# An opening ordered by hand, with heads in 126 columns and rows placed by stores

## The chip, the cores and the metric

One core of a Trainium2 chip runs the kernel. The metric is the device time of one execution in microseconds, as the median over runs.

## The reference

The computation is the forward pass and the gradients of a gated mix of two attention branches, on 2048 tokens of width 576 in bfloat16. Only branch A and the gate matter for this change:

```python
# A: 32 query heads of 18, one key and value head for all of them
q = (x @ wq).reshape(B, S, 32, 18).transpose(0, 2, 1, 3)
k, v = x @ wk, x @ wv
p = softmax(einsum('bhqd,bkd->bhqk', q, k) * 18 ** -0.5)
a = einsum('bhqk,bkd->bhqd', p, v)...reshape(B, S, 576) @ wo
# B: segments of 32 tokens with 8 memory rows carried from one to the next, 32 heads of 128
g = sigmoid((x * gate_w).sum(-1, keepdims=True))
out = g * a + (1 - g) * b
# and the gradients for x, wq, wk, wv, wo, mem0, Wq, Wk, Wv, Wo, gate_w from grad_out
```

For its backward pass branch A needs, per head, q and the gradient of the head's output: `da = g * grad_out` times the transpose of `wo`. Branch B needs `db = (1 - g) * grad_out`.

## The kernel before

The kernel is a row of stages, each with its own pools of SBUF and PSUM: an opening; the transposed weight Wo of branch B (`make_WoT`); the token projections of branch B (`b_proj`); branch A's forward sweep woven with B's chain over the segments; B's bulk work; A's second sweep woven with B's backward chain; the weight gradients; the end. The change lies in the opening and adds small stores to `b_proj`.

**The opening before.** `prep` loads x and grad_out as tokens by features (`xt`, `go`, 16 tiles of 128 tokens), transposes x into `xT` on TensorE (five 128 x 128 transposes a tile, evacuated by ScalarE), and takes the gate's dot product on VectorE (line 1601). When all 16 dots are there, one Exp gives the gate for all tokens (line 1609). Then it scales `go` by g into `xt` and by 1 - g into itself (line 1619), transposes both (`daT`, `dbT`), and stores xT, da, db and dbT to DRAM for later stages. `a_weights` loads Wq, Wk, Wv and Wo of branch A; it spreads each head's 18 columns over 32 (`wqp`, `woTp`: 16 pairs of heads, 64 columns a pair). `a_setup` makes the keys and values as columns (`KV`) and as rows (`VK`, `WK`) and from the largest key of each feature a weight `smneg`.

`a_qd_all` then runs over 16 pairs of heads and 4 blocks of 512 tokens. For one unit, TensorE fills rows 0 to 63 of one PSUM tile `a_pq` with q of the pair and rows 64 to 127 with its output gradient, five steps of the contraction each, side by side in the two column halves of the array. ScalarE takes the absolute value of it (line 1756), and one more product with `smneg` adds for each token and head a lower bound, - |q| times the largest keys, in row 18 of each group of 32 rows; the softmax later needs no maximum. VectorE casts the tile to `a_QDs` (line 1766, three buffers), and one store takes all 128 rows, zero rows among them, to `qs_dram` (line 1767; even blocks from SyncE's queue, odd ones from GpSimd's). In `qs_dram` a head pair and block has 128 rows of 512 values, of 1 KB each:

```
rows   0-17  q, first head     18  its bound     19-31  zero
rows  32-49  q, second head    50  its bound     51-63  zero
rows  64-81  output gradient, first head         82-95  zero
rows 96-113  output gradient, second head       114-127 zero
```

`setup_A_consts` and `setup_B_consts` make masks and selection matrices, mostly on GpSimd, and `load_Wo` loads Wo of branch B (4.7 MB, half from each queue). In this stage the instructions of each engine are put in order by a scheduler; the stages behind it have an order written out by hand (`tc.manual_schedule()`), in which each engine runs its instructions as the program lists them.

**Behind it.** `proj_load` loads tiles `p_x` of dbT and xT. `make_WoT` transposes Wo (`w_ptr`, `WoT`) and stores it (line 637). `b_proj` does 31 items of 128 tokens: products into eight PSUM tiles `p_pb`, evacuated by VectorE and ScalarE to `p_tok` (line 77 and 79, two buffers), stored by SyncE one item later (lines 239 and 258). Its function `extra(n)` is called at item n and loads Wk and Wv at items 1 to 10 and Wq at item 16, then first memory rows and `load_A_kv`, which begins to read `qs_dram`. `load_v` (line 392) loads a tile `c_vx` in the sweep behind: 32 tokens by 4096 values, taken as "r (c x) -> c r x" with four groups c.

A TensorE, VectorE, ScalarE or GpSimd instruction whose line is a helper's carries that line: 82 for all products, 87 for transposes by `tr`, 77 and 79 for `evac` on VectorE and ScalarE.

Of the kernel before, what the change touches and what calls it, by code (L numbers as in the profile page):

```python
# [10 lines left out]
ALU = mybir.AluOpType  # L11
# [5 lines left out]
P = 128  # L17
# [29 lines left out]
class Kern:  # L47
# [1528 lines left out]
    def prep(self, keep, xk, sp, psum):  # L1576
        nc = self.nc
        T, NTT = self.T, self.NTT
        gwb = sp.tile([P, D], BF16, name="gwb")
# [3 lines left out]
        self.xT = xk.tile([P, NKT, T], BF16, name="xT")  # L1583
        self.daT = xk.tile([P, NKT, T], BF16, name="daT")
        dbT = sp.tile([P, NKT, T], BF16, name="dbT")
# [3 lines left out]
        for dst, src in ((xt, self.A_x), (go, self.grad_out)):  # L1589
            for q in range(4):  # L1590
                n0, n1 = q * NTT // 4, (q + 1) * NTT // 4
                nc.sync.dma_start(dst[:, n0:n1, :], src[n0 * P:n1 * P, :].rearrange("(n p) d -> p n d", p=P))
        xl = sp.tile([P, NTT, 2, 4, 16], BF16, name="xtail")
        tail_in = lambda t: t.rearrange("p (g c) -> p g c", c=GD)[:, :, P:GD].unsqueeze(1).to_broadcast([P, 2, 4, 16])
        tail = lambda tt: xl[:, tt].rearrange("p a g c -> p (a g c)")
        z = sp.tile([P, NTT], F32, name="z_all")
        for tt in range(NTT):
            for a in range(2):
                nc.scalar.copy(xl[:, tt, a], xt[:, tt, :].rearrange("p (g c) -> p g c", c=GD)[:, :, P:GD])
            junk = sp.tile([P, D], BF16, name="junk", bufs=2)  # L1600
            nc.vector.tensor_tensor_reduce(out=junk[:], in0=xt[:, tt, :], in1=gwb[:], scale=1.0, scalar=0.0,
                                           op0=ALU.mult, op1=ALU.add, accum_out=z[:, tt:tt + 1])
            tp = psum.tile([P, 6, P], BF16, name="trx", bufs=4)
            for kt in range(4):
                nc.tensor.transpose(tp[:, kt, :], xt[:, tt, GD * kt:GD * kt + P], self.identB[:])
            nc.tensor.transpose(tp[:, 4, :], tail(tt), self.identB[:])
            self.evac(self.xT[:, :, tt * P:(tt + 1) * P], tp[:, 0:5, :], use="s")
        ez = sp.tile([P, NTT], F32, name="ez")
        nc.scalar.activation(ez[:], z[:], ACT.Exp, scale=-1.0)
        nc.vector.tensor_scalar(out=ez[:], in0=ez[:], scalar1=1.0, scalar2=None, op0=ALU.add)  # L1610
        nc.vector.reciprocal(self.g_all[:], ez[:])
        nc.vector.tensor_scalar(out=self.omg_all[:], in0=self.g_all[:], scalar1=-1.0, scalar2=1.0,
                                op0=ALU.mult, op1=ALU.add)
        for kt in range(NKT):
            nc.gpsimd.dma_start(self.xT_dram[kt], self.xT[:, kt, :])
        for (dst, gcol, ddram, d4) in ((self.daT, self.g_all, self.da_dram, xt), (dbT, self.omg_all, self.db_dram, go)):
            for tt in range(NTT):
                d16 = d4[:, tt, :]
                nc.vector.tensor_scalar(out=d16, in0=go[:, tt, :], scalar1=gcol[:, tt:tt + 1], scalar2=None,
                                        op0=ALU.mult)  # L1620
                if tt % 4 == 3:
                    nc.gpsimd.dma_start(ddram[(tt - 3) * P:(tt + 1) * P, :].rearrange("(n p) d -> p n d", p=P), d4[:, tt - 3:tt + 1, :])
                tp = psum.tile([P, 6, P], BF16, name="trx", bufs=4)
                step = GD if dst is dbT else P
                for kt in range(4):
                    nc.tensor.transpose(tp[:, kt, :], d16[:, kt * step:kt * step + P], self.identB[:])
                if dst is dbT:
                    nc.gpsimd.tensor_copy(xl[:, tt], tail_in(d16))
                    nc.tensor.transpose(tp[:, 4, :], tail(tt), self.identB[:])
                else:  # L1630
                    nc.tensor.transpose(tp[:, 4, :], d16[:, D - P:D], self.identB[:])
                self.evac(dst[:, :, tt * P:(tt + 1) * P], tp[:, 0:5, :], use="v" if tt % 3 == 2 else "s")
        for kt in range(NKT):
            nc.gpsimd.dma_start(self.dbT_dram[kt], dbT[:, kt, :])

    def a_weights(self, keep, sp, psum):
        nc = self.nc
        wq = sp.tile([P, NKT, D], BF16, name="a_wq")
        wo = sp.tile([P, NKT, D], BF16, name="a_wo")
        wkv = keep.tile([P, NKT, P], BF16, name="a_wkv")  # L1640
        nc.gpsimd.memset(wkv[:], 0.0)
        self.wkv36 = keep.tile([P, NKT, 36], BF16, name="a_wkv36")
        for kt in range(NKT):
            rows = KT_ROWS[kt]
            r = slice(kt * P, kt * P + rows)
            nc.gpsimd.dma_start(wo[0:rows, kt, :], self.A_wo[r, :])
            for p0, n, r0 in d_rows(kt):
                nc.sync.dma_start(wq[p0:p0 + n, kt, :], self.A_wq[r0:r0 + n, :])
                nc.sync.dma_start(self.wkv36[p0:p0 + n, kt, 0:DA], self.A_wk[r0:r0 + n, :])
                nc.sync.dma_start(self.wkv36[p0:p0 + n, kt, DA:36], self.A_wv[r0:r0 + n, :])  # L1650
        for kt in range(NKT):
            rows = KT_ROWS[kt]
            for i in range(4):
                c0 = (i // 2) * DA
                nc.gpsimd.tensor_copy(wkv[0:rows, kt, 32 * i:32 * i + DA], self.wkv36[0:rows, kt, c0:c0 + DA])
        self.wkv = wkv
        self.wqp = keep.tile([P, NKT, NPR, 64], BF16, name="a_wqp")
        self.woTp = keep.tile([P, NKT, NPR, 64], BF16, name="a_woTp")
        nc.vector.memset(self.wqp[:], 0.0)
        nc.gpsimd.memset(self.woTp[:], 0.0)  # L1660
        for kt in range(NKT):
            rows = KT_ROWS[kt]
            nc.vector.tensor_copy(
                self.wqp[0:rows, kt, :, :].rearrange("p n (i c) -> p (n i) c", c=32)[:, :, 0:DA],
                wq[0:rows, kt, :].rearrange("p (h e) -> p h e", e=DA))
        for kd in range(NKT):
# [77 lines left out]
    def a_qd_all(self, sp, psum):  # L1744
        prev = None
        for p in range(NPR):
            for qb in range(self.T // 512):
# [9 lines left out]
                if prev is not None:  # L1757
                    self.a_qd_end(*prev, sp)
# [504 lines left out]
```

## Time and profile before

| | us |
|---|---|
| median of 3 runs | 5326.19 |
| lowest, highest | 5325.88, 5336.03 |
| profiled execution, own time | 5334.26 |
| its span, first to last instruction | 5332.5 |

The mean granted TensorE clock of the profiled execution was 0.986. A line that groups instructions reads: line, engine, operation, output <- inputs, shape, count | busy us, mean ns of one | idle us of that engine just before them, and what ended it. A line of the timeline reads: start us, us, engine, line, operation, tiles, count, and in brackets the idle time before and what ended it. PEld is the load of weights into the array; SPq is SyncE's queue of DMA issues.

### The profile page before, as it was taken

How to read it: one execution, taken by the hardware profiler on the slowest of the kernel's cores; microseconds unless marked ns; L12 is line 12 of the kernel's file. 1: busy time of each engine (PE TensorE's matmuls, PEld its weight loads, DVE VectorE, ACT ScalarE, POOL GpSimd, SP SyncE). 2: the span in 40 equal slices, each digit the busy share in tenths (PEclk: the TensorE clock that was granted, in tenths of full speed). 3: DMA queues.
4: the chain of work that ended last, by engine and by line, in shares of the span. 5: the costliest groups of instructions: out<-in, count | busy, mean ns of one | idle time of the engine just before them, and what ended most of it. 6: DMA issues, size and time to landing. Idle time of an engine off the chain costs nothing. (4 is left out here: it accounts for less than half of the span.)

```text
span 5332.5 us, 214646 instructions
## 1 busy us (share of the span) xinstructions
PE 5036.9 (94%) x91428; PEld 2940.1 (55%) x91428; DVE 3610.4 (68%) x7146; ACT 3321.1 (62%) x4816; POOL 2576.9 (48%) x4890
## 2 busy tenths in 40 slices
PE   7999999999999998999889999999999999999999
PEld 6434555555555555777645555555544467764444
DVE  5337888888888887777678888888888831111112
ACT  4327888888888886666668888878877732111101
POOL 4004555555555555777746666666654321222223
PEclk9999999999999999999999999999999999999999
DMA  6645666656655445888867999899987778976653
GB/s 220 230 178 132 147 142 141 139 144 141 141 146 130 117 113 175 252 256 250 256 180 172 202 196 195 193 190 194 195 173 140 149 163 225 267 230 211 196 174 116
DMA packets 1115762, 961.21 MB, mean 180 GB/s; under 512 B 690738, under 2 KB 942139, under 8 KB 1105202
## 3 DMA queue, kind: packets, MB, share of 16 engines
q1 hardware_dynamic: 1013730, 702.18, 54.6%
q0 software_dynamic: 100928, 245.16, 15.7%
q8 instruction: 715, 11.71, 1.0%
q14 instruction: 245, 2.01, 0.1%
q10 hardware_dynamic: 144, 0.15, 0.0%
HBM read 521.16 MB, written 357.96 MB: 165 GB/s over the span
## 5 line engine op out<-in xcount | busy, mean ns | idle before, releaser
L1982 DVE TENSOR_TENSOR b_dS<-b_dP,b_E 128x512 bf16<-128x512 f32 x2048 | 1314.1, 683 | 235.6 <-issue 97.4
L1819 DVE TENSOR_TENSOR a_W<-a_dP,a_E 128x512 bf16<-128x512 f32 x2048 | 1313.3, 683 | 206.7 <-issue 74.6
L1959 ACT ACTIVATE b_E<-b_S 128x1024 bf16<-128x1024 f32 x1024 | 1047.8, 1023 | 298.5 <-PE b_dP L82 209.1
L1786 ACT ACTIVATE a_E<-a_S 128x1024 bf16<-128x1024 f32 x1024 | 1049.0, 1024 | 239.8 <-PE a_dP L82 192.6
L82 PEld LDWEIGHTS <-b_QS 32*128 32x128 bf16 (+1 forms) x8192 | 269.4, 92 | 529.8 <-issue 461.4
L82 PE MATMUL r_pj<-WT,r_dT 128*32 128x288 bf16 x12288 | 498.0, 287 | 8.4 <-issue 8.3
L82 PE MATMUL b_S<-b_KV,b_QS 32*128 32x512 bf16 x2048 | 406.6, 385 | 97.9 <-ACT b_E L1959 58.9
L82 PE MATMUL w_acc<-w_d,w_h 128*128 128x512 bf16 (+1 forms) x2400 | 473.8, 379 | 0.0
L82 PE MATMUL a_S<-a_QD,l_KV 32*128 32x512 bf16 x2048 | 399.5, 381 | 43.0 <-ACT a_E L1786 21.0
L82 PE MATMUL b_acc<-b_dS,b_QS 128*32 128x512 bf16 x2048 | 425.9, 394 | 0.2
L82 PE MATMUL a_acc<-a_E,l_VK 128*32 128x256 bf16 x8192 | 412.7, 278 | 5.2
L82 PE MATMUL b_acc<-b_E,b_QS 128*32 128x512 bf16 x2048 | 409.5, 395 | 1.5 <-issue 1.5
L82 PE MATMUL b_dP<-b_KV,b_QS 32*128 32x512 bf16 x2048 | 404.5, 390 | 0.0
L82 PE MATMUL a_dP<-a_QD,l_KV 32*128 32x512 bf16 x2048 | 398.4, 385 | 0.1
L82 PEld LDWEIGHTS <-r_dT 128*32 128x32 bf16 x12288 | 336.9, 97 | 100.7 <-issue 14.4
L82 PEld LDWEIGHTS <-w_h 128*128 128x128 bf16 (+1 forms) x2688 | 229.9, 100 | 258.4 <-issue 6.6
L82 PEld LDWEIGHTS <-l_KV 32*128 32x128 bf16 x4096 | 150.2, 91 | 288.5 <-issue 264.6
L82 PE MATMUL a_acc<-a_W,l_WK 128*32 128x256 bf16 x4096 | 291.4, 273 | 0.4 <-DVE a_W L1819 0.3
L79 ACT CAST w_o<-w_acc 128x512 bf16<-128x512 f32 x54 | 31.6, 585 | 384.3 <-PE w_acc L82 358.0
L77 DVE CAST w_o<-w_acc 128x512 bf16<-128x512 f32 x54 | 37.3, 691 | 335.2 <-PE w_acc L82 306.8
L82 PEld LDWEIGHTS <-l_VK 128*32 128x32 bf16 x8192 | 129.3, 94 | 237.1 <-issue 233.3
L1100 POOL TENSOR_TENSOR r_kb<-r_ks,bmask 128x512 bf16<-128x512 bf16 x176 | 188.7, 1072 | 146.6 <-DMA r_ks<-px_dram 59.1
(484 smaller groups left out, 10798.6 us busy)
## 6 DMA issues: line engine op xcount, KB each, us to landing
b_QS<-qs_dram SPq DMA_DIRECT2D x256, 256.0 KB
dOx_dram<-p_tok SPq DMA_DIRECT2D x16, 1024.0 KB
c_vx<-vx_dram SPq DMA_DIRECT2D x64, 256.0 KB
krow_dram<-c_k POOLq DMA_DIRECT2D x64, 256.0 KB
qrow_dram<-c_q POOLq DMA_DIRECT2D x64, 256.0 KB
vrow_dram<-c_v POOLq DMA_DIRECT2D x64, 256.0 KB
x_q<-qx_dram SPq DMA_DIRECT2D x32, 512.0 KB
x_k<-kx_dram SPq DMA_DIRECT2D x32, 512.0 KB
```

Of the source, the lines that this page charges most:

```text
L77: nc.vector.tensor_copy(out, in_)
L79: nc.scalar.copy(out, in_)
L82: return self.nc.tensor.matmul(out, lhsT, rhs, start=start, stop=stop, tile_position=tp, skip_group_check=True)
L1100: nc.gpsimd.tensor_tensor(out=B[:], in0=a[:].unsqueeze(2).to_broadcast([P, 4, 4, SEG]), in1=self.bmask[:, :, 0].unsqueeze(1).unsqueeze(3). ...
L1786: nc.scalar.activation(E_[n][:], S.pop(n)[:], ACT.Exp, scale=SCALEA)
L1819: nc.vector.tensor_tensor(out=W_[n][:, i, :], in0=dP[i][:], in1=E_[n][:, i, :], op=ALU.mult)
L1959: nc.scalar.activation(E_[n][:], S.pop(n)[:], ACT.Exp, scale=SCALEA)
L1982: nc.vector.tensor_tensor(out=D_[n][:, i, :], in0=dP[i][:], in1=E_[n][:, i, :], op=ALU.mult)
```

## The change

The three functions `prep`, `a_weights` and `a_setup`, the head loop `a_qd_all` and the constants become one function `prep` under `tc.manual_schedule()`.

- **Heads in 126 columns.** Wq and the transposed Wo are laid out as even heads, then odd heads, 18 columns a head without gaps (`wqd`, `woT`). `proj` takes seven heads (126 columns; four in the last of five blocks) by 512 tokens, either q ("q") or the output gradient ("d"): 20 units each.
- **Rows placed by stores.** SyncE stores each unit's rows to their places in `qs_dram`, heads outermost, 18 rows a head; a block whose heads lie in both halves takes two stores. The buffers `a_QDs` are six.
- **The bound** of a block of 512 tokens is made for all 32 heads by five products with `smd` into `a_pb` (`bound`), and stored as 2 x 16 rows. `largest` spreads the largest keys to 126 rows with one product by `rep`.
- **The gate in two parts** of eight tiles (`gates`), the dots spread over the order. The keys come in four blocks with a largest value each (`keys`).
- **The order:** x tiles with five q units and three key blocks between them; then a loop over units 5 to 39 with one gated tile, one transposed tile and other parts after each. dbT goes to DRAM in four pieces. Wo's load stands behind the x tiles. The tail copies of x move from ScalarE to GpSimd.
- **Constants last:** `setup_B_consts` is the last call, `setup_A_consts` stands early.
- **Zero rows:** `qs_pads` stores the zero rows from a zero tile at items 11 to 26 of `b_proj`, two stores an item.

The diff, cut to its core:

```diff
+        def proj(w, u):
+            qb, b = u // 5, u % 5
+            W, X = (wqd, xT) if w == "q" else (woT, daT)
+            k0, k1 = 7 * b, min(7 * b + 7, 32)
+            m = DA * (k1 - k0)
+            pq = psum.tile([P, 512], F32, name="a_pq", bufs=4)
+            for kt in range(NKT):
+                self.mm(pq[0:m, :], lhsT=W[:, kt, DA * k0:DA * k1], rhs=X[:, kt, qb * 512:qb * 512 + 512],
+                        start=(kt == 0), stop=(kt == NKT - 1))
+            st = sp.tile([P, 512], BF16, name="a_QDs", bufs=6)
+            if w == "q":
+                absq[u] = sp.tile([P, 512], BF16, name="a_absq", bufs=12)
+                nc.scalar.activation(absq[u][0:m, :], pq[0:m, :], ACT.Abs)
+                nc.vector.tensor_copy(st[0:m, :], pq[0:m, :])
+            else:
+                self.evac(st[0:m, :], pq[0:m, :], use="sv"[u % 2])
+            for i in range(2):
+                lo, hi = max(k0, 16 * i), min(k1, 16 * i + 16)
+                if lo < hi:
+                    r0 = 32 * i + (0 if w == "q" else 64)
+                    nc.sync.dma_start(
+                        self.qs_dram[lo - 16 * i:hi - 16 * i, qb, r0:r0 + DA, 0, :], st[DA * (lo - k0):DA * (hi - k0), :])
+
+        def keys(q):
+            lo = 512 * q
+            pk = psum.tile([P, 512], F32, name="a_pq", bufs=4)
...
+            nc.vector.tensor_scalar(out=KV[:, lo:lo + 512], in0=pk[:], scalar1=self.onesrow[:, 0:1], scalar2=None, op0=ALU.add)
+            absk = sp.tile([64, 512], BF16, name="a_absk", bufs=2)
+            nc.scalar.activation(absk[:], KV[0:64, lo:lo + 512], ACT.Abs)
+            nc.vector.tensor_reduce(out=mk4[:, q:q + 1], in_=absk[:], axis=AX.X, op=ALU.max)
...
+        def bound(qb):
+            pb = psum.tile([32, 512], F32, name="a_pb", bufs=1)
+            for b in range(5):
+                m = DA * min(7, 32 - 7 * b)
+                self.mm(pb[:], lhsT=smd[0:m, b, :], rhs=absq.pop(5 * qb + b)[0:m, :], start=(b == 0), stop=(b == 4))
+            bn = sp.tile([32, 512], BF16, name="a_bn", bufs=2)
+            nc.scalar.copy(bn[:], pb[:])
+            for i in range(2):
+                nc.sync.dma_start(self.qs_dram[:, qb, 32 * i + DA, 0, :], bn[16 * i:16 * i + 16, :])
...
+        dots = iter(range(NTT))
+        for tt in range(NTT):
+            if tt % 4 == 0:
+                for a in range(2):
+                    nc.gpsimd.tensor_copy(xl[:, tt:tt + 4, a], ...)
...
+            turn(xt[:, tt, :], tail(tt), tt, GD, xT[:, :, tt * P:(tt + 1) * P], "s")
+            if tt in (5, 7, 10, 12, 14):
+                proj("q", (5, 7, 10, 12, 14).index(tt))
+            if tt in (6, 9, 13):
+                keys((6, 9, 13).index(tt))
+            if tt % 2 == 1:
+                gate_dot(next(dots))
+        for kt in range(NKT):
+            nc.gpsimd.dma_start(self.xT_dram[kt], xT[:, kt, :])
+        self.load_Wo(bwo)
...
+        gates(0)
...
+        for u in range(5, 40):
+            for d in itertools.islice(dots, 2 if u % 2 else 1):
+                gate_dot(d)
+            if u == 10:
+                gates(1)
+            proj("q" if u < 20 else "d", u % 20)
+            if u == 6:
+                keys(3)
+                nc.sync.dma_start(self.kv_dram[:, :], KV[:, :])
+            if u == 8:
+                largest()
+            if u < 10:
+                wo_turn(u - 5)
+            if u >= 7 or u == 5:
+                for x in itertools.islice(ahead, 1):
+                    gated(*x)
+                for x in itertools.islice(tiles, 1):
+                    gated_T(*x)
+            if u in (10, 12, 16, 21):
+                bound((10, 12, 16, 21).index(u))
+            if u in (36, 37, 38, 39):
+                tok_kv(u - 36)
...
+        nc.sync.dma_start(self.vk_dram[0], VK[:])
+        nc.sync.dma_start(self.vk_dram[1], WK[:])
+        self.setup_B_consts(keep)
+
+    def qs_pads(self, n, sp):
...
+        for k in range(2 * n, 2 * n + 2):
+            r0, nr = ((19, 13), (51, 13), (82, 14), (114, 14))[k // 8]
+            p0 = 8 * (k % 2)
+            self.nc.sync.dma_start(self.qs_dram[p0:p0 + 8, k // 2 % 4, r0:r0 + nr, 0, :], self.z512[0:8 * nr, :])
...
-    def a_qd_all(self, sp, psum):
...
-        with SB("xk") as xk, SB("a1k") as a1k, SB("a1s") as a1s:
-            with SB("p0s") as p0s, PS("p0ps") as p0ps:
-                k.prep(cpool, xk, p0s, p0ps)
-                k.a_weights(a1k, a1s, p0ps)
...
+        with tc.manual_schedule(), SB("xk") as xk, SB("a1s") as a1s, PS("a1p") as a1p:
+            k.prep(cpool, bwo, xk, a1s, a1p)
...
                 def extra(n):
                     if 1 <= n <= 10:
                         k.load_W("kv"[(n - 1) // 5], (n - 1) % 5)
+                    if n >= 11:
+                        k.qs_pads(n - 11, pds)
...
                         def extra(n):
+                            if n < 27:
+                                k.qs_pads(n - 11, pds)
                             if n == n0:
```

`turn` transposes a tile by five products into `trx` (three buffers) and evacuates it; `gated` scales a tile by g or 1 - g and, every fourth tile, stores da or db from GpSimd's queue; `gated_T` turns the gated tile into daT or a piece of dbT; `wo_turn` transposes a block of branch A's Wo; `tok_kv` makes VK and WK for four tiles.

More of the change, by code (lines that the diff above doesn't have):

```diff
@@ L1589, in prep @@
[L1589 to L1592, printed above, removed]
+        wq = sp.tile([P, NKT, D], BF16, name="a_wq")
+        wo = sp.tile([P, NKT, D], BF16, name="a_wo")
+        wqd = sp.tile([P, NKT, D], BF16, name="a_wqd")
+        woT = sp.tile([P, NKT, D], BF16, name="a_woT")
+        wkv36 = sp.tile([P, NKT, 36], BF16, name="a_wkv36")
@@ L1608, in prep @@
[L1608 to L1666, printed above, removed]
@@ new lines, in prep @@
+        for kt in range(NKT):
+            nc.gpsimd.dma_start(self.xT_dram[kt], xT[:, kt, :])
+        self.load_Wo(bwo)
+        nc.gpsimd.memset(VK[:], 0.0)
+        nc.gpsimd.memset(WK[:], 0.0)
+        nc.gpsimd.memset(VK[:, :, DA:DA + 1], 1.0)
+        nc.gpsimd.memset(WK[:, :, 37:38], 1.0)
+        gates(0)
+        side = [("a", tt) for tt in range(NTT)] + [("b", tt) for tt in range(NTT)]
+        ahead = iter(side)
+        gated(*next(ahead))
+        tiles = iter(side)
+        for u in range(5, 40):
[20 more added lines that the diff above has]
+                tok_kv(u - 36)
```

207 lines of the change are left out of this document (123 added, 84 removed).

## The prediction

> **What bounds the kernel now.** I read the head and the engine totals of the page first, then one table of windows cut at the stages around the change, then the groups of instructions of the first 220 us by shape, then the timeline at the hand-overs, and last the waits and the DMA issues.
>
> ```profile
> span 5332.5 us, 214646 instructions
> PE 5036.9 (94%) x91428; PEld 2940.1 (55%) x91428; DVE 3610.4 (68%) x7146; ACT 3321.1 (62%) x4816; POOL 2576.9 (48%) x4890
> ```
>
> The columns of the windows are: length, busy us of PE, weight loads, DVE, ACT and POOL (with instruction counts), granted clock, DMA share, GB/s.
>
> ```profile
> 0.00:56.00 56.00, 31.86 (x315) 25.20 (x316) 35.46 (x93) 31.78 (x75) 42.93 (x139) 0.88 0.97 310
> 0.00:80.00 80.00, 53.23 (x504) 38.53 (x506) 46.55 (x115) 40.70 (x91) 47.56 (x151) 0.89 0.90 297
> 56.00:148.00 92.00, 88.75 (x756) 66.69 (x756) 47.15 (x74) 39.96 (x69) 18.75 (x39) 0.98 0.41 145
> 100.00:120.00 20.00, 20.00 (x174) 16.70 (x171) 10.72 (x16) 9.46 (x16) 4.24 (x8) 1.00 0.29 101
> 148.00:162.50 14.50, 11.11 (x161) 10.13 (x160) 7.82 (x18) 9.63 (x18) 2.87 (x5) 0.88 0.60 241
> 300.00:320.00 20.00, 20.00 (x99) 7.69 (x97) 6.44 (x10) 5.37 (x10) 0.00 (x0) 1.00 0.86 324
> 424.00:425.00 1.00, 1.00 (x16) 0.18 (x12) 0.25 (x1) 0.00 (x0) 1.00 (x2) 0.50 0.25 92
> ```
>
> The opening has two halves. Up to 56 us the DMA engines are full (0.97) and no compute engine is above 43 of 56 us. From 56 to 148 us TensorE works 88.75 of 92 us on the head projections while DMA is at 0.41. Behind it the stages follow one another: TensorE makes the transposed Wo (to 162.5 us) and is then full in the token projection (20.00 of 20.00). So an opening that ends earlier moves everything behind it.
>
> ```profile
> 12.48 0.76 DVE L1601 CUSTOM_DVE_ANT_0 junk<-xtok,gwb 128x576 bf16<-128x576 bf16 x1 [1.39 <-DMA xtok<-in_A_x_dram]
> 25.62 0.23 ACT L1609 ACTIVATE ez<-z_all 128x16 f32<-128x16 f32 x1
> 32.96 0.40 PE L1626 MATMUL trx<-identB,xtok 128*128 128x128 bf16 x4
> 33.24 0.39 PE L1626 MATMUL trx<-identB,xtok 128*128 128x128 bf16 x4
> 60.43 1.35 PE L82 MATMUL a_p<-a_wkv,xT 128*128 128x36 bf16 x20
> 133.97 0.69 DVE L1766 CAST a_QDs<-a_pq 128x512 bf16<-128x512 f32 x1 [0.60 <-PE a_pq L82]
> 135.27 0.69 DVE L1766 CAST a_QDs<-a_pq 128x512 bf16<-128x512 f32 x1 [0.60 <-PE a_pq L82]
> 147.66 0.38 PE L82 MATMUL a_pq<-a_absq,a_smneg 128*64 128x512 bf16 x1 [0.54 <-ACT a_absq L1756]
> 151.25 0.76 DVE L77 COPY WoT<-w_ptr 128x512 bf16<-128x512 bf16 x2 [2.48 <-DMA qs_dram<-a_QDs]
> 162.51 3.62 PE L82 MATMUL p_pb<-WoT,p_x 128*128 128x512 bf16 x16
> ```
>
> **The change, part by part: TensorE.** A unit of the old projection is two heads by 512 tokens: five passes in which q fills one column half and the output-gradient half the other, then one pass for the bound. The casts at 133.97 and 135.27 us stand 1.30 us apart, so a pass costs 0.216 us, and 64 units cost 83 us. The new form packs seven heads in 126 columns: 20 units for q and 20 for the gradient, five passes each (200), and 20 passes for the bounds: 220 x 0.216 = 47.5 us instead of 83.
>
> ```profile
> L1766 DVE CAST a_QDs<-a_pq 128x512 bf16<-128x512 f32 x64 | 44.1, 691 | 42.6 <-PE a_pq L82 31.3 <-DMA qs_dram<-a_QDs 11.3
> L1756 ACT ACTIVATE a_absq<-a_pq 128x512 bf16<-128x512 f32 x64 | 38.2, 597 | 48.8 <-PE a_pq L82 48.8
> L1601 DVE CUSTOM_DVE_ANT_0 junk<-xtok,gwb 128x576 bf16<-128x576 bf16 x16 | 11.0, 751 | 5.8 <-DMA xtok<-in_A_x_dram 5.8
> L79 ACT COPY xT<-trx 128x640 bf16<-128x640 bf16 x16 | 9.9, 719 | 0.0
> L1599 ACT COPY xtail<-xtok 128x64 bf16<-128x64 bf16 x32 | 5.4, 254 | 8.6 <-DMA xtok<-in_A_x_dram 8.6
> L1619 DVE TENSOR_SCALAR xtok<-gotok,g_all 128x576 bf16<-128x576 bf16 x16 | 4.9, 364 | 0.0
> L82 PE MATMUL a_p<-xT,a_wkv 128*128 128x512 bf16 x20 | 4.5, 378 | 0.0
> L1685 DVE TENSOR_SCALAR a_KV<-a_p,a_onesrow 128x512 bf16<-128x512 f32 x4 | 3.0, 751 | 2.3 <-PE a_p L82 2.3
> L1692 DVE TENSOR_REDUCE a_mk<-a_absk 64x1 f32<-64x2048 bf16 x1 | 2.3, 2279 | 2.0 <-ACT a_absk L1690 2.0
> L77 DVE COPY dbT<-trx 128x640 bf16<-128x640 bf16 x5 | 2.4, 489 | 4.8 <-PE trx L1629 4.7
> L77 DVE COPY a_woTp<-a_wtr 128x576 bf16<-128x576 bf16 x2 | 0.9, 454 | 0.2 <-PE a_wtr L87 0.2
> L155 POOL TENSOR_SCALAR_AFFINE_SELECT maskZ<-maskZ 128x32 f32<-128x32 f32 x8 | 2.4, 302 | 0.3
> ```
>
> **The new order, stage by stage.** *To the end of the x transposes.* The old kernel is there at 25.62 us (the gate's Exp comes behind them). Wq now loads between the first two quarters of x, 0.66 MB at 310 GB/s = 2 us, and five q units and three key blocks are slipped in, which ScalarE must serve (5 x 0.60, and three abs at a quarter of the old size). The rows let me place it between 25.6 and 32 us; I take 28, since ScalarE also loses the 32 small tail copies (5.4 us) to GpSimd.
> *Units 5 to 9.* VectorE now holds more than TensorE: eight gate dots at 0.68 (11.0 us / 16), five casts at 0.69, five turned Wo blocks at 0.45, four gated tiles at 0.36, one key block (0.75 and a quarter of 2.28), the largest-key step and the half gate, about 2: 5.5 + 3.5 + 2.3 + 1.5 + 1.3 + 2 = 16 us. Ends at 44.
> *Units 10 to 19.* TensorE has per unit 5 x 0.216 and one tile of five transposes (0.28, the distance of the rows at 32.96 and 33.24), and three bounds: 13.6 + 3.2 = 17 us. VectorE has 0.69 + 0.36 per unit and ScalarE 0.60 + 0.72, just below TensorE's 1.36. Ends at 61.
> *Units 20 to 39.* 20 x 1.08, 18 tiles at 0.28, one bound and four key/value blocks at 1.35: 21.6 + 5.0 + 1.1 + 5.4 = 33 us. VectorE and ScalarE share casts and copies and stay under 1 us per unit. Paced by TensorE the opening would thus end at 94 to 95 us, not 148.
>
> **DMA.** The spread-out traffic stays the same: to 80 us the share of 0.90 makes 72 us of all sixteen engines; about ten old head stores in it go out of the account. The row at 100 to 120 us, where only those stores run, gives 0.29 x 16 x 20 / 2.02 MB = 46 engine-us per MB, or 47 ns per 1 KB row; ten stores of 128 rows are 3.8 us, leaving 68.2. New head rows: 40 x 126 and 128 of bounds, 5168 in all, 15.2 us if spread evenly. Then the end would be at 2 + 68 + 15 = 85 us, behind TensorE.
>
> Whether they spread is the open cost: a new store has heads (7, 5, 4 or 2 of them) as its outer axis, 18 rows each, where the old one had 128 rows. The nearest row is the load of c_vx, whose source has four row groups outermost:
>
> ```profile
> 418.75 0.97 SPq L392 DMA_DIRECT2D c_vx<-vx_dram  x1
> ...
> c_vx<-vx_dram SPq DMA_DIRECT2D x64, 256.0 KB
> ```
>
> It was issued at 418.75 us and is alone under way at 424 to 425 us, where the share is 0.25 and 92 GB/s flow: four of sixteen engines. So I let a store run on as many engines as it has heads, 18 rows on each. What no row shows is whether these are always the same engines. If they rotate, it is the 15.2 us above. If not, the busiest engine takes a part of every store (six for each of eight groups of five units, since the block that crosses the halves needs two): 48 x 18 + 8 = 872 rows, 41 us, and is done at 2 + 68 + 41 = 111 us. I take this end, since one queue with one shape of transfer gives no reason to rotate in any row; both ends go into the range. With about six stores queued (the new buffers) TensorE ends some 3 us before it, at 108.
> The Trainium skill, page "DMA: Bandwidth & Descriptors", section "Why a DMA increments its semaphore by 16 and not by 1", says that the engine count is the largest number up to 16 that divides both sides' slowest axis, and that SyncE's queue takes the lowest-numbered ones. The c_vx row agrees on the count; by the page the sum would be 108, by rotation 95, and no run here shows the numbering.
>
> **Small edits.** GpSimd's masks move to the end; VectorE's one cast waits for them. Eight selects at 0.30 and some thirty smaller ones make about 7 us, started after the last gated store, some four units (6 us or more) before TensorE ends: nothing, or up to 7 us in front of the Wo evacuations if that cover is gone. Wo's load moves behind the x stage; its 4.7 MB are in the 68 us and have 70 us to land. The hand-over to Wo, 147.9 to 151.25 us, waits for the last head stores, and will again: unchanged. SyncE now holds all head stores; behind each waiting one stand later stores, the transposed gradient and the first p_x loads, which have the Wo stage (14.5 us) as cover.
> The zero rows, 32 stores of 104 or 112 rows (outer axis 8), are 27 rows or 1.3 us of eight engines per item, beside DMA shares of 0.4 to 0.6. Only where Wq loads (0.86 at 300 to 320 us) is it tight:
>
> ```profile
> DVE p_tok L77 <- DMA kx_dram<-p_tok: 5.4, 1, 5.4
> DVE a_QDs L1766 <- DMA qs_dram<-a_QDs: 11.3, 6, 6.3
> ACT a_absk L1690 <- DVE a_KV L1685: 4.3, 1, 4.3
> DVE a_mk L1692 <- ACT a_absk L1690: 2.0, 1, 2.0
> ```
>
> VectorE waits there 5.4 us for a token store behind that load, and TensorE stays full; two items of zero rows lengthen it by up to 2.6 us. I charge 1 us (0 to 2.6).
>
> **Sum.** 148 - 108 = 40 us gained, 1 lost: 39 us. The profiled execution took 5334.26 us (span 5332.5); the median of the runs shown is 5326.19, 8.1 lower. Against its own time 5295, against the median **5287 us**. A difference of 0.2% (10.7 us) is what a measurement of this kernel can tell from none.
>
> **Rivals.**
> *TensorE paces* (head stores spread or hidden): end at 95, gain 53 - 1, 5274 us. For it: even traffic of 85 us. Against it: the c_vx row. Chance 0.22.
> *The order by hand stalls*: each engine runs in program order, and a key block goes TensorE, VectorE, ScalarE, VectorE. Its waits in the rows above, 4.3 / 4 + 2.0 = 3.1, come four times (12.4), and one wait for a store of the longest kind, 6.3, is added since SyncE's queue holds Wo's 2.4 MB ahead of the stores: 108 + 19 = 127, gain 20, 5306 us. For it: with three buffers the old order already waited 11.3 us; against it: now six buffers. Chance 0.18.
> *Fewer engines still* (slower): if a store uses one engine whatever its heads, that engine has 5168 rows, 243 us; the opening ends at 2 + 68 + 243 - 3 = 310, 5326 + 162 + 1 = 5489 us. Two engines are 121 us, 188, 5367 us. It decides from 80 us on the busiest engine, 1700 rows, twice my count. For it: nothing in the trace has an outer axis of 7. Against it: c_vx keeps all four. Chance 0.10.
> *No change*: 1475 to 1930 rows on the busiest engine (80 us and 10.7 us to either side), or the full stalls of both kinds (127 plus 7 for the masks, and one more 6.3): chance 0.08. That the change does not do what it says, with the passes staying at 384, the code excludes.
>
> **How the numbers follow.** The forecast has 0.42. Its own range is 5279 (VectorE's stages partly hidden) to 5297. Faster: 0.42 + 0.22 + 0.18 = 0.82; same 0.08; slower 0.10. The range 5266 to 5314 takes in the forecast, TensorE's pace less 8 us for an earlier x stage, and the stalls with 8 us more; outside lie the slower cases.
>
> **What would show it.** Right: 220 passes of a_pq and a_pb of about 0.216 us; the first p_pb pass at about 123 us; VectorE or TensorE waiting on `qs_dram<-a_QDs` between 50 and 105 us; a DMA share under 1 while stores queue (few engines full). First p_pb at 110 us with no such waits means TensorE paces; idle before a_mk or a_absk of 10 us and more means the order stalls. The prediction is wrong if p_pb starts after 148 us, or if the gain at p_pb is lost again before 420 us.

## The result, and the profile after

The changed kernel takes 5298.43 us in the median of four runs (5284.42 to 5305.19), the kernel before 5330.31 us in four runs beside them: 31.9 us less, a ratio of 0.9935 with a 95% interval of 0.9921 to 0.9948. The forecast was 5287 us, its range 5266 to 5314. The profiled execution took 5284.42 us. It is the fastest of the four, so its whole span says less than its stages; from here on both kernels are compared by the start of their stages.

| us in the profiled executions | before | after | gained so far |
|---|---|---|---|
| last a_pq pass of the opening | 147.7 | 115.8 | 31.9 |
| first p_pb pass (token projection) | 162.5 | 128.4 | 34.1 |
| first pass of the forward sweep | 417.7 | 387.7 | 30.0 |
| span | 5332.5 | 5282.7 | 49.8 |

The last 19.8 us of the last row come from stages that the change does not touch. The longest piece of them, from the first `b_S` pass to the first `y_pk` pass, took 1671 us before and 1650 after; in the profiles of the twelve experiments, which leave it alone too, it took 1646 to 1670. I count the change as 30 us; the medians, 31.9 us apart, agree with that.

The head and the engine totals of the changed kernel's page:

```profile
span 5282.7 us, 213348 instructions
PE 4991.7 (94%) x90766; PEld 2902.2 (55%) x90945; DVE 3589.8 (68%) x7122; ACT 3293.3 (62%) x4757; POOL 2553.9 (48%) x4852
```

TensorE is 45 us lighter, 33 of them ahead of the forward sweep (352.8 us busy there, 386.0 before); the other 12 lie in stages that the change leaves alone. The groups of its instructions up to 130 us, by shape, show the new passes (count, busy us, mean ns of one, idle time before them):

```profile
L82 PE MATMUL a_pq<-xT,a_wqd 128*126 128x512 bf16 x80 | 23.2, 426 | 0.0
L82 PE MATMUL a_pq<-daT,a_woT 128*126 128x512 bf16 x80 | 21.1, 397 | 0.0
L82 PE MATMUL a_pq<-xT,a_wqd 128*72 128x512 bf16 x20 | 6.1, 443 | 0.0
L82 PE MATMUL a_pq<-daT,a_woT 128*72 128x512 bf16 x20 | 5.3, 398 | 0.0
L82 PE MATMUL a_pb<-a_absq,a_smd 126*32 126x512 bf16 x16 | 5.0, 443 | 0.0
L82 PE MATMUL a_pb<-a_absq,a_smd 72*32 72x512 bf16 x4 | 1.8, 444 | 0.0
```

These are 200 and 20 passes, the forecast's 220. Passes of one group start 0.216 us apart in the median, as forecast. The windows of the opening, cut at its stages (length, busy us of PE, weight loads, DVE, ACT, POOL, granted clock, DMA share, GB/s), show where the time is now:

```profile
8.00:32.00 24.00, 17.92 (x129) 11.61 (x127) 14.10 (x28) 14.01 (x24) 5.72 (x16) 1.00 0.75 222
32.00:52.00 20.00, 13.02 (x68) 7.54 (x70) 17.38 (x46) 6.12 (x12) 7.46 (x12) 0.75 0.96 329
52.00:77.00 25.00, 20.96 (x116) 10.83 (x115) 9.36 (x22) 13.14 (x24) 1.51 (x2) 0.86 0.55 189
77.00:116.00 39.00, 35.76 (x276) 22.63 (x275) 17.57 (x43) 14.81 (x26) 14.09 (x59) 0.96 0.60 187
116.00:128.40 12.40, 10.18 (x161) 8.71 (x160) 8.00 (x21) 9.28 (x18) 5.60 (x27) 1.00 0.77 254
```

Up to 14 us TensorE awaits x tiles (2.50 of 6 us busy from 8 on); from 14 to 32 us it is busy for 15.42 of 18. From 32 to 52 us VectorE is the bound, 17.38 of 20. From 52 to 77 us no engine is full, and DMA stands at 0.55: the order waits for something. From 77 to 116 us TensorE works 35.76 of 39 us; nearly all that it lacks lies between 90 and 100 us, where it works 7.10 of 10. The granted clock is 0.75 and 0.86 from 32 to 77 us, so the passes that follow a wait are also slower. Some of the waits from 30 to 130 us (engine, line, what was awaited: us, times, longest):

```profile
DVE a_QDs L1664 <- ACT a_absq L1663: 12.3, 9, 5.1
POOL w_tail L641 <- DMA vk_dram<-a_WK: 6.3, 1, 6.3
ACT a_absk L1681 <- DVE a_KV L1679: 5.1, 2, 4.2
DVE a_QDs L1664 <- DMA qs_dram<-a_QDs: 4.7, 1, 4.7
PE a_pq L82 <- DVE a_mk L1686: 4.7, 1, 4.7
DVE a_dbT L77 <- DMA dbT_dram<-a_dbT: 3.7, 1, 3.7
ACT a_dbT L79 <- DMA dbT_dram<-a_dbT: 3.6, 1, 3.6
```

Some of these at their place in time, with GpSimd's memsets and SyncE's issues from the same stretch behind the first row, and the start of the token projection as the last:

```profile
36.22 2.45 DVE L1719 TENSOR_SCALAR xtok<-gotok,g_all 128x576 bf16<-128x576 bf16 x1
36.53 0.97 POOL L1790 MEMSET a_VK<- 128x1024 bf16 x1
37.42 0.97 POOL L1791 MEMSET a_WK<- 128x1024 bf16 x1
35.97 17.04 SPq L1671 DMA_DIRECT2D qs_dram<-a_QDs  x2
46.40 0.16 PE L82 MATMUL a_pq<-a_mk,a_rep 64*126 64x1 bf16 x1 [4.72 <-DVE a_mk L1686]
59.23 0.69 DVE L1664 CAST a_QDs<-a_pq 126x512 bf16<-126x512 f32 x1 [4.74 <-DMA qs_dram<-a_QDs]
98.17 0.49 DVE L77 COPY a_dbT<-trx 128x640 bf16<-128x640 bf16 x1 [3.69 <-DMA dbT_dram<-a_dbT]
128.45 1.90 PE L82 MATMUL p_pb<-WoT,p_x 128*128 128x512 bf16 x7
```

Two stores keep SyncE for 17.04 us behind Wo's load; at 59.23 us the cast of unit 11 waits until the buffer of unit 5 is stored. The waits and the timeline of the token projection show what the zero rows cost:

```profile
ACT p_tok L79 <- DMA kx_dram<-p_tok: 9.5, 1, 9.5
DVE p_tok L77 <- DMA kx_dram<-p_tok: 9.3, 1, 9.3
287.03 5.30 PE L82 MATMUL p_pb<-Wk,p_x 128*128 128x512 bf16 x16 [1.89 <-ACT p_tok L79]
287.00:292.00 5.00, 4.97 (x16) 1.89 (x15) 1.90 (x4) 1.45 (x3) 0.00 (x0) 0.66 0.76 252
```

The wait for the token store has grown to 9.3 us from 5.4, TensorE now waits 1.89 us for it, and the block behind it takes 5.30 us at a granted clock of 0.66. From the first p_pb pass to the sweep it is 259.3 us, where it was 255.2.

### The profile page after: what moved, and what is told of

Same layout as the page of the kernel before. It is cut to its first block, busy times and chain, and to the rows that moved or that the text cites. A ratio compares the mean times of both kernels' runs of the same rounds, so it can differ in the third digit from the quotient of the medians.

```text
span 5282.7 us, 213348 instructions
## 1 busy us (share of the span) xinstructions
PE 4991.7 (94%) x90766; PEld 2902.2 (55%) x90945; DVE 3589.8 (68%) x7122; ACT 3293.3 (62%) x4757; POOL 2553.9 (48%) x4852
## 4 chain that ended last, share of the span: by engine, by line
PE 69%; ACT 9%; issue 8%; DVE 5%; DMA 4%; POOL 4%; SPq 1%; POOLq 0%; ACTq 0%; DVEq 0%
PE w_acc L82 12%; PE r_pj L82 7%; PE b_S L82 6%; PE a_S L82 6%; PE a_acc L82 5%; ACT b_E L2052 5%; PE c_pj L82 5%; PE b_acc L82 5%; PE r_x L82 5%; PE p_pb L82 4%; PE c_x L82 4%; ACT a_E L1879 3%; PE x_tr L87 2%; PE f_big L82 1%; PE x_po L82 1%
## 5 line engine op out<-in xcount | busy, mean ns | idle before, releaser
L82 PE MATMUL a_S<-a_QD,l_KV 32*128 32x512 bf16 x2048 | 399.3, 381 | 41.6 <-ACT a_E L1879 19.8
```

Of the source, the lines that this page charges most:

```text
L82: return self.nc.tensor.matmul(out, lhsT, rhs, start=start, stop=stop, tile_position=tp, skip_group_check=True)
```

## The experiments

The theory after the result: a store side (SyncE's queue and the few engines that a head store uses) sets the pace behind 52 us, VectorE the stretch before. The rivals: TensorE paces; the order by hand stalls by itself; the number of stores counts, not their shape. "p_pb" below is the start of the first p_pb pass, 128.4 us in the changed kernel; "last a_pq" is 115.8 there. Stage times come from one profile each. A whole time with a ratio is a median of four to ten runs beside 23 runs of the kernel before (nine in the last experiment); one given beside another time is a single run beside a single run.

**Store cut by heads, or by columns.**

```
+ mid = (lo + hi) // 2
+ for a, b_ in ((lo, mid), (mid, hi)):
      nc.sync.dma_start(self.qs_dram[a - 16*i:b_ - 16*i, ...], st[DA*(a - k0):DA*(b_ - k0), :])
# control
+ for c in (slice(0, 256), slice(256, 512)):
      nc.sync.dma_start(self.qs_dram[..., 0, c], st[..., c])
```

> Each head store is cut in two by heads (3 and 4 instead of 7). The bytes stay, the stores go from 48 to 96, and each half again puts 18 rows of 1 KB on every engine it uses. Theory (every head store begins on the same few DMA engines, and the busiest one bounds the opening): the busiest engine's rows double from 872 to 1736, 41 us more on it; about 30 us of that show, so the first pass of the token projection moves from 128.4 to 150 - 165 us, and VectorE waits for head stores to land for 20 us or more. Rival A (only SyncE's issues cost, 0.6 us each): 48 more issues are 29 us of SyncE, which has slack; under 5 us later. Rival B (stores rotate over the engines): the same rows on average, no change, 127 to 131 us.

> The control: each head store is cut in two by columns, 2 x 256 values. As many issues as with the heads split (96), but each half has seven heads and rows of 512 bytes, so the busiest engine keeps its bytes. Theory (busiest engine): its 864 rows become 1728 halves; if a half costs half a row nothing changes (128 - 132 us), if it costs up to 0.7 of a row the first pass of the token projection comes up to 12 us later (140). Rival A (issues cost): as late as with the heads split. Rival B: 127 to 131 us.

Measured: by heads 5315.15 us, ratio 0.9975 (0.9962 to 0.9988), last a_pq at 131.4, p_pb at 142.9; by columns 5301.64 us, ratio 0.9949 (0.9933 to 0.9966), last a_pq at 126.3, p_pb at 139.2. Both are later than the changed kernel, by 14.5 and 10.8 us at p_pb. The cut by heads is the dearer, as the theory wants, and not in one profile alone: the medians of ten and of four runs lie 13.5 us apart. But its p_pb misses the theory's 150 to 165, and 10.8 of the 14.5 us come with the control too, which has twice as many stores of rows half as long. Over the whole kernel the control's interval overlaps the changed kernel's, that of the cut by heads does not.

**Extra stores, flat or by heads.** Forty more stores of 64 rows into the second slot of the rows, which the opening leaves free; once with the rows outermost, once with four heads of 16 rows.

```
+ nc.sync.dma_start(self.qs_dram[u % 16, qb, (64 if w == "d" else 0):(128 if w == "d" else 64), 1, :], st[0:64, :])
# or
+ nc.sync.dma_start(self.qs_dram[4*(b%4):4*(b%4)+4, qb, r:r+16, 1, :], st[0:64, :])   # r: 16 rows in each of four heads
```

> Each of the 40 units also stores 64 rows of its tile (64 KB) to a part of the same DRAM tensor that is written again later; the rows lie one behind another, so the outer axis is 64. Forty more issues and 2.6 MB more. Theory (an outer axis of 64 spreads over all engines): 4 rows an engine, 160 rows on each, 5 to 8 us of work; the first token-projection pass 0 to 6 us later than 128.4. If it is the issue on SyncE's queue that delays: 8 us or more later, and the same as in the next run.

> The same 40 extra stores of the same 64 rows, but laid out as four heads of 16 rows, so the outer axis is 4. Same bytes, same row length, same number of issues as the run before. Theory (outer axis 4 means four engines, and always the same ones as the head stores use): 16 rows more per unit on each of them, 640 in all, 480 more than in the run before; 5 to 15 us later than that run, with more waiting for qs_dram and dbT stores. Rival (engines rotate, or only issues cost): within 2 us of that run.

Measured: flat 5314.45 us, last a_pq 125.3, p_pb 137.0; by heads 5312.38 us, last a_pq 131.0, p_pb 143.3. So at p_pb 6.3 us for the shape, and 8.6 for forty stores that were expected to cost 0 to 6. SyncE's issues (count; ns least, median, most; from 60 to 130 us) in the flat one, the head stores and the extra ones:

```profile
L1671 SPq DMA_DIRECT2D qs_dram<-a_QDs x38: 667/768/1661, 60.8 to 128.6; - x38
L1673 SPq DMA_DIRECT2D qs_dram<-a_QDs x33: 509/520/1643, 60.0 to 129.3; - x33
```

An issue of a head store takes 0.67 us at least here. The old flat store took half of that, from 30 to 145 us in the kernel before:

```profile
L1767 SPq DMA_DIRECT2D qs_dram<-a_QDs x30: 332/332/468, 67.4 to 142.7; - x30
```

Forty extra issues of 0.52 are 21 us of SyncE. That is a price which the prediction left out. It also means that in these four kernels SyncE's own time is part of the bound, so they measure the shape less cleanly than meant. The extra stores by heads took 0.58 us to issue in the median, so 2 of the 6.3 us can be SyncE's as well.

**Every product twice.** 200 passes more (43 us at 0.216), stores as they are; each contraction runs through and then starts over in the same tile.

```
- for kt in range(NKT):
+ for kt in range(2 * NKT):
+     kt %= NKT
```

> Every head unit's five products are done twice over (the second set starts the sum anew), so TensorE has 200 passes more of 0.216 us, 43 us. Theory (TensorE paces units 10 to 39, other engines or stores only add a few stalls): 25 to 38 us later, the first token-projection pass at 153 - 166 us. Rival (stores and VectorE pace the whole opening, TensorE's passes are free): less than 15 us later, under 143 us.

Measured: 5309.23 us, ratio 0.9963 (0.9953 to 0.9973); last a_pq at 139.1, p_pb 22.1 us later. The window of its last units, and SyncE's head stores from 90 to 118 us, there first and in the changed kernel below:

```profile
77.00:116.00 39.00, 39.00 (x237) 24.45 (x236) 13.29 (x32) 12.93 (x22) 5.91 (x14) 1.00 0.44 143
L1672 SPq DMA_DIRECT2D qs_dram<-a_QDs x13: 652/760/782, 90.1 to 115.8; - x13
L1671 SPq DMA_DIRECT2D qs_dram<-a_QDs x17: 662/1320/2217, 90.5 to 116.7; - x17
```

With TensorE full (39.00 of 39.00), no head store is awaited and an issue takes 0.76 us. In the changed kernel the same issue takes 1.32 in the median, while the DMA engines on average are at 0.60: the queue takes stores more slowly than SyncE could issue them. The 22.1 us lie between the theory's 25 and the rival's 15: TensorE gave half of what it was charged, so it sets the pace in about half of the opening. The run also parts the gain: with 420 passes, more than the 384 of the kernel before, p_pb still comes at 150.5 us, 12.0 before the old 162.5. So some 22 of the 34 us are the passes', the rest the new order's.

**Odd units' stores from GpSimd's queue.**

```
- nc.sync.dma_start(
+ (nc.gpsimd if u % 2 else nc.sync).dma_start(
```

> Every second unit's head stores go from GpSimd's queue instead of SyncE's. Theory (SyncE's stores share the lowest engines): if GpSimd's queue spreads its stores over other engines, the busiest engine loses about half of 864 rows, 20 us; the two waits for landed head stores (4.7 and 1.5 us) and the one for a dbT piece (3.7) go, with the slow clock behind them about 10 us: first token-projection pass at 117 - 122 us instead of 128.4. Rival (order and GpSimd's own issue time of 0.54 us each are what counts): GpSimd's issues delay the tail copies and da stores behind them, 128 - 134 us.

Measured: 5302.09 us, ratio 0.9956 (0.9943 to 0.9969), last a_pq at 119.8, p_pb at 139.5. The waits for dbT's stores are gone, but GpSimd's order now stands behind the casts and gated tiles, and its list of constants comes late; DVE's mask and the Wo evacuations wait for it (from 104 to 145 us):

```profile
DVE maskX L159 <- POOL maskZ L157: 7.8, 1, 7.8
PE w_ptr L87 <- DVE WoT L77: 7.3, 1, 7.3
```

Nor is p_pb in the theory's 117 to 122 or the rival's 128 to 134. The rival's way is seen at the start: the tail copies come late, and the x transposes end at 35.9 us instead of 31.8. From there to the last a_pq it takes 83.9 us, 84.0 in the changed kernel. A queue moved is an order moved: the try does not tell the store side's price, but it shows the mask's.

**Twelve store buffers, four for dbT.**

```
- name="a_QDs", bufs=6     + name="a_QDs", bufs=12
- name="a_dbT", bufs=2     + name="a_dbT", bufs=4
```

> Twelve buffers for the head tiles instead of six and four for the dbT pieces instead of two, nothing else. Theory (the busiest DMA engine only shows through full buffers): the waits of 4.7 and 1.5 us for head stores and of 3.7 us for a dbT piece vanish, with the slow clock behind two of them; the first token-projection pass at 117 - 122 us. Rival (VectorE's stretch and TensorE pace): 126 - 128.5 us.

Measured: 5293.98 us beside 5325.97; last a_pq at 105.7, ten us earlier, p_pb at 123.2, five earlier and a little behind the theory's 117 to 122. Its window of the last units, and the wait behind them (95 to 125 us):

```profile
77.00:106.00 29.00, 29.00 (x251) 19.52 (x250) 15.26 (x38) 11.45 (x20) 12.89 (x57) 1.00 0.67 207
POOL w_tail L641 <- DMA vk_dram<-a_WK: 10.7, 1, 10.7
```

Now TensorE is full to the end at clock 1.00, and no head unit waits for a store any more. So such waits cost the opening of the changed kernel ten us: units 10 to 19 take 20.8 us here instead of 26.6, and what follows 32.9 instead of 37.8. Half of the gain is lost again at once: the copies of Wo's tail use the room of WK, whose store stands last in SyncE's queue, so Wo's stage takes 17.4 us instead of 12.5. The issue of a head store did not get faster (1.32 us in the median from 90 to 118 us, as before); the wait moved to the next consumer of its queue.

**Memsets of VK and WK early.**

```
- nc.gpsimd.memset(VK[:], 0.0) ...          # behind the x transposes
+ if tt == 1: nc.gpsimd.memset(VK[:], 0.0) ...
```

> The zeroing of VK and WK on GpSimd is moved from behind the x transposes to the second x tile. Theory (the GpSimd memsets hold VectorE's gate product of 2.45 us at 36 us, where its like take 0.36 to 0.62): the first gated tile takes 0.7 us or less, units 5 to 9 end 1 to 2.5 us earlier than at 51.4 us, the first p_pb pass at 126 to 128 us. Rival (that product was late for another reason): it takes over 2 us again, and nothing moves by more than 0.5 us up to unit 9.

Measured: 5288.1 us beside 5345.57. The gated tile at the same place in VectorE's timeline:

```profile
36.08 0.47 DVE L1719 TENSOR_SCALAR xtok<-gotok,g_all 128x576 bf16<-128x576 bf16 x1
```

2.45 us have become 0.47: GpSimd's memsets held it. Unit 9's cast ends at 49.2 instead of 51.4. By unit 14 nothing is left of that (68.1 against 68.5), and the last a_pq comes at 122.6, later than in the changed kernel. The cast of unit 11 waits 7.1 us for a store here, 4.7 there: what VectorE gives is taken by the stores. The expected p_pb at 126 to 128 came at 135.3.

**All gate products with the x tiles.**

```
- if tt % 2 == 1:
-     gate_dot(next(dots))
+ gate_dot(next(dots))
```

> All sixteen gate products of x run one by one with the x tiles, instead of eight there and eight in units 5 to 10. Theory (VectorE paces units 5 to 9, busy for 17.4 of 20 us, and has room before): 8 products of 0.75 us = 6 us leave that stretch; it ends 3 to 6 us earlier than at 51.4 us, and the opening 0 to 5 us earlier than at 115.8 us, since what follows also waits for stores. Rival (the x stretch has no room: VectorE there is held by the x loads): the x transposes end 3 us or more later than at 31.8 us and unit 9 within 1 us of where it was.

Measured: 5294.14 us beside 5345.57. Unit 9 ends at 49.6, 1.8 us earlier; the x transposes end 2.5 us later (34.3). Neither theory hits: VectorE had room, but not for free. Its windows:

```profile
8.00:32.00 24.00, 18.53 (x125) 11.68 (x124) 17.05 (x38) 11.78 (x20) 7.36 (x16) 1.00 0.73 217
32.00:52.00 20.00, 13.73 (x88) 7.70 (x86) 14.68 (x40) 10.04 (x18) 7.29 (x12) 0.91 0.85 293
```

Here, too, the last a_pq is late (122.0) and a cast waits 8.3 us for a head store. Two kernels that change no store thus end the opening 6 to 7 us later than the changed one. Whether their order does that or chance is not settled: the one other kernel with the same opening (the zero rows' below) ends it at 117.1 instead of 115.8, with the same p_pb. So the 6.3 us for the shape above, from one profile each, are not shown to be the shape's.

**The constants first again.**

```
  self.setup_A_consts(keep)
+ self.setup_B_consts(keep)
...
- self.setup_B_consts(keep)
```

> The list of constants that the changed kernel puts behind the last stores (11 us of GpSimd there) is put back right behind the first constants. Theory of the prediction (the masks are hidden wherever they stand): the first p_pb pass within 2 us of the changed kernel's 128.4 us. Rival (the first copies of the x tails queue behind the list on GpSimd): the first tail copy comes at about 20 us instead of 9, the first a_pq pass 8 to 11 us later than 15.7 us, and of that 3 to 11 us are left at the first p_pb pass.

Measured: 5308.07 us beside 5345.57; first a_pq pass at 23.9 instead of 15.7, last a_pq at 126.4, p_pb at 138.8, so 10.4 us later. The rival is right. The wait on TensorE between 8 and 32 us:

```profile
PE trx L1649 <- POOL xtail L1773: 12.7, 1, 12.7
```

The first copies of the x tails stand behind the list on GpSimd. Placing the constants last is worth 8 us at the start, once the tail copies are GpSimd's; the prediction had that at nothing.

**The zero rows clear of Wq's load.** Four an item, at items 11 to 14 and 20 to 23.

```
- if n >= 11: k.qs_pads(n - 11, pds)
+ if 11 <= n <= 14: k.qs_pads(2*n - 22, pds); k.qs_pads(2*n - 21, pds)
# and the same at 20 to 23 in place of n < 27
```

> The zero rows are stored at items 11 to 14 and 20 to 23, four stores an item, so none stands in SyncE's queue around the load of Wq (items 16 to 19). Theory (two items of zero rows behind and ahead of Wq lengthen the wait for a token buffer from 5.4 to 9.5 us, past what PSUM covers): the stretch from the first token-projection pass to the first pass of the sweep, 259.3 us, falls back to 255 to 256 (255.2 before). Rival (the whole projection is slower because of 27 zero rows an item, wherever they stand): stays at 258 to 260.

Measured: 5293.06 us beside 5325.97; p_pb at 128.4 as before, the sweep at 383.6: 255.2 us between them, as in the kernel before the change and as the theory says (255.3 in the next experiment, which has the same edit; 257.2 to 260.9 in the ten others). The waits are back to its size:

```profile
ACT p_tok L79 <- DMA kx_dram<-p_tok: 5.6, 1, 5.6
DVE p_tok L77 <- DMA kx_dram<-p_tok: 5.4, 1, 5.4
```

**All together.** The buffers, the zero rows, the memsets and the gate products as above, and the token keys at units 28 to 34 with their stores behind unit 36.

```
- if u in (36, 37, 38, 39): tok_kv(u - 36)
+ if u in (28, 30, 32, 34): tok_kv((u - 28) // 2)
+ if u == 36: nc.sync.dma_start(self.vk_dram[0], VK[:]); nc.sync.dma_start(self.vk_dram[1], WK[:])
```

> Together: twelve store buffers and four of dbT, the zero rows at items 11 to 14 and 20 to 23, the memsets of VK and WK at the second x tile, all gate products with the x tiles, and the token keys at units 28 to 34 with their stores behind unit 36. Theory (with buffers enough, what is saved at VectorE in units 5 to 9 stays; the copies of Wo's tail no longer wait for the WK store): unit 9 ends by 50 us, the last a_pq pass at 100 to 105 us, Wo's stage in 11.5 to 13 us, the first p_pb pass at 112 to 118 us, the token projection 255 us, the whole 5262 to 5280 us beside 5330 before. Rival (the rows in store set the end whatever VectorE does): the last a_pq pass at 105 us or later and the first p_pb pass at 119 us or later, the whole 5281 to 5293 us.

Measured: 5285.57 us (5274.8 to 5292.79), ratio 0.9923 (0.9909 to 0.9936). Last a_pq 105.4, p_pb 123.4, sweep 378.7: nine us before the changed kernel's sweep. The interval overlaps the changed kernel's, so its lead over that is likely and not shown. The times are the rival's: no gain in the opening beyond that of the buffers. Its cause is not shown, since TensorE is busy for 28.96 of the 29 us from 77 to 106 us. The wait for WK is gone, and Wo's stage still takes 17.8 us. Its waits from 104 to 125 us, and TensorE's timeline:

```profile
DVE maskX L159 <- POOL maskZ L157: 4.3, 1, 4.3
ACT WoT L79 <- POOL maskZ L155: 4.8, 1, 4.8
111.56 9.74 PE L87 MATMUL w_ptr<-identB,WoN 128*128 128x128 bf16 x112 [4.22 <-DVE WoT L77]
```

GpSimd's list starts when the last gated tile is stored, 103 us here, and is not done when the opening ends at 105.4; VectorE's mask waits for it and the Wo evacuations behind it.

## Why the prediction was right, and which terms were off

The sign, the place and most of the size are as forecast: 220 passes instead of 384 (some 22 of the 34 us at p_pb, by the doubled products), the opening ending some 30 us earlier, and no second loss behind it beyond the zero rows. The sum was 39 us; 30.0 were left at the sweep. The median, 5298.43, lies 11 us above the forecast, just outside its own range (to 5297), and 8 us below the rival of the stalls (5306): the whole time alone would not tell them apart, the stages must. That the opening's end is off by only 8 us (115.8 for 108) is in part luck: by unit 19 the order is 17 us late, and 9 of these come back behind it.

- **To the end of the x transposes**, 28 forecast, 31.8 measured (range 25.6 to 32). TensorE waits 2.1 us for the second quarter of x, which is there at 13.75 us, 1.4 us later than in the kernel before (12.39); that is near the 2 us taken for Wq. More weighs what was charged to ScalarE alone, the five q units and three key blocks slipped in: from 14 to 32 us TensorE is busy for 15.42 of 18 us, in 12.23 of them with these.
- **Units 5 to 9**, 16 us forecast, 19.6 measured (31.8 to 51.4). VectorE was rightly the bound (17.38 of 20). Missing were one gated tile of 2.45 us instead of 0.36, held by GpSimd's memsets, and the waits inside: TensorE stands 4.72 us for `a_mk`, ScalarE 4.2 for the key block. Moving the memsets or the gate products away ended unit 9 about 2 us earlier.
- **Units 10 to 19**, 17 forecast as TensorE's, 26.6 measured (to 78.0): 4.74 us for a store behind Wo's load, and a granted clock of 0.86 in its window. That is the second rival's price; it came once and not at full size. With buffers enough they take 20.8 us.
- **Units 20 to 39**, 47 forecast to 108, the stores pacing; 37.8 measured to 115.8. The waits for stores came where they were foretold, together with a DMA share of 0.60. With enough buffers the stage takes 32.9 us (72.8 to 105.7), the forecast's 33 for TensorE. So the stores add 4.9 us to this stage, where the forecast had them add 14, and 10 to the whole opening.
- **The stores' term.** "872 rows by 47 ns on the busiest engine" was put as the cause, with 111 us as the end. The last head store was issued at 116.7. The runs bear out that the stores hold the opening up and that more of them, by heads above all, end later. They bear out the working only in part: SyncE's issue, 0.65 to 0.77 us for a head store where nothing stands in front and 1.32 in the median behind 90 us, was not in the sum at all.
- **Few engines.** That a store keeps to few engines can be counted in the trace, from the start and length of each 1 KB packet of SyncE's queue. In the kernel before, from 100 to 120 us, 10.5 are in flight on average while any is, and more than 7 in 67% of the time. In the changed kernel, from 110 to 114.8 us, where only head stores are issued, 4 on average, and more than 7 in 4% of the time. And from 84 to 118 us the queue has packets in flight for 97% of the time, so there it is no less full than TensorE (30.6 of 34 us). The Trainium skill, page "DMA: Bandwidth & Descriptors", section "Why a DMA increments its semaphore by 16 and not by 1", gives a store the largest number of engines up to 16 that divides both sides' slowest axis. The trace agrees on few engines; which ones they are it does not hold, so whether it is always the same ones, and how the price splits between engines and issue, stays open. One count was off besides: every fifth unit has 72 rows and not 126, so the rows with the bounds are 4736 instead of 5168 (13.9 us if spread evenly, 223 on one engine); the forecast itself does not use it.
- **Wo's hand-over** was forecast unchanged at 14.5 us; it is 12.5, a gain of 2 that was not foreseen. **The masks** were charged at nothing, or up to 7 us without cover: nothing in the changed kernel, 7.3 and 4.2 us in the two kernels that took the cover away.
- **The zero rows** were charged 1 us, at most 2.6. They cost 4.1: the longer wait of VectorE was foreseen, that TensorE would run dry for 1.9 us and be slower behind it (5.30 instead of 3.63 us) was not.

Of the rivals, TensorE's pace (95) is refuted as the pace of the whole opening by the end at 115.8 and by the doubled products; the order's stalls (127) appear as 4.2 to 4.7 us waits before `a_absk`, behind `a_mk` and for one store, below the ten that were named as their sign, but they are much of what the forecast missed by unit 19; fewer engines (310) did not happen.

## What to carry to other kernels

A transfer that is hidden by its bytes can still bound a stage by its issue: count the instructions of the one queue that holds them, read their time from SyncE's rows, and compare it with the pace of the stage. A gain at one engine passes on only when the next resource has room: here VectorE's 2 us, half of the buffers' 10 us and the earlier WK store each ran into the next wait, and each wait showed in one line of the view. Small stores put beside a tight load should stand where the load isn't.

## What the runs showed of the hardware

- A VectorE product on bfloat16 tiles took 2.45 us while GpSimd wrote two memsets of 0.97 us each, and 0.47 with them moved away. The Trainium skill, page "SBUF — State Buffer", section "SBUF: two separate sides", says that a VectorE instruction in a two-port mode and a GpSimd instruction exclude each other from a shared port pair, and that the one which starts first has it to its end. This trace agrees that the product waited, by 2 us: it ended at 38.67 us, the memsets at 37.50 and 38.39. That the first one wins it does not show, since the product's record begins 0.31 us before the first memset's; nor does a row tell the mode.
- SyncE's issue of a store with 2 to 7 heads of 18 rows took 0.65 to 0.87 us where nothing stood in front, that of 128 flat rows 0.33. Behind the load of Wo one issue lasted 12.17 us.
- After waits of TensorE of 1.9 to 4.7 us the granted clock was 0.66 to 0.86 in the windows around them. At 287 us a short wait so cost nearly twice its length: 1.9 us of waiting, and 1.7 us more for the 16 passes behind it (5.30 instead of 3.63).
